# Transposing normalised tiles by DMA instead of by the tensor array: layernorm, dilated attention and a gated feed-forward on one core

## Chip, cores, metric

One NeuronCore of a Trainium2 chip. The metric is the device time of one execution in microseconds (us); medians over several executions are quoted, with lowest and highest; these take in the runs classed as slow (one of the run with the array kept busy, two of the run with the early load alone), the ratios do not. "Before" and "after" are the kernel without and with the change.

## The reference

```python
S, D, H, F = 2048, 448, 16, 1792                  # bfloat16
xn = layernorm(x)                                 # (S, D)
q, k, v = split(xn @ wqkv)                        # 16 heads of 28
# each position attends to 8 positions: itself and 2, 4 .. 14 before it
s = softmax(q . k * 28**-0.5, masked) @ v @ wo
g = silu(gelu(xn @ w1 + b1) @ w2 + b2)
return x + s * g
```

The rows are held as even positions and then odd ones, so that the dilated window becomes a plain one. They are worked in four chunks of 512 (four tiles of 128 rows each).

## The kernel before

All matmuls that read `xn` take it from a buffer with features on the partitions. So every normalised tile (`xnb`, 128 rows by 512 columns, four buffers used in turn) is transposed by the array (TensorE, PE in profiles) into a PSUM buffer (`pT`) and copied into one feature-major buffer `xnT`.

```python
LEAD = 8                                          # columns of zeros ahead of xnT
...                                               # loads, all issued from the SP queue
nc.sync.dma_start(b1t[:], B_b1.rearrange("(m f) -> f m", f=P))
for c0, c1 in ((0, F // 2), (F // 2, F)):
    ...                                           # half of w1
    if c0 == 0:
        nc.sync.dma_start(x_sb[1][:, :, :], dram_rows(x_par, 4, 4))
...                                               # w2, b2, x_sb[2], x_sb[3]
for g in range(4):
    for h in range(4):                            # sixteen small pieces of wo
        r = (4 * g + h) * DH
        nc.sync.dma_start(wo[32 * h + 1:32 * h + 1 + DH, g, :], A_wo[r:r + DH, :])

def ln_tr(t):                                     # four array transposes of one tile
    pT = psB.tile([P, KT, P], BF16, name="pT", tag="B")
    for kt in range(KT):
        nc.tensor.transpose(pT[:, kt, :], xnb[t % 4][:, kt * P:(kt + 1) * P], ident[:])
    return pT

def ln_put(t, pT, copy):
    copy(xnT[:, :, LEAD + t * P:LEAD + (t + 1) * P], pT[:, :, :])

def feed_forward_1(c, ps, wos):                   # chunk c; seven pairs of blocks, k = 0 .. 6
    ...
    for k in range(0, MT // 2, 2):
        ...                                       # matmuls and gelu of pairs k and k + 1
        if k in (2, 4):
            if c + 1 < NC:                        # transposes of the NEXT chunk
                for j in (k - 2, k - 1):
                    ln_put(nx + j, ln_tr(nx + j), nc.vector.tensor_copy)
            ...
        for _ in range(2):                        # output projections of finished tiles
            if k >= (2 if c == 3 else 4) and wos:
                wo_job(wos.pop(0))
```

The order of the array, VectorE, ScalarE and GpSimd is fixed by hand to the order of the program. The queue on the sync engine (SP), which issues nearly all DMAs, is left to the scheduler.

The softmax here doesn't subtract the row's maximum and nothing guards it: scores larger than these inputs give would overflow.

Of the kernel before, what the change touches and what calls it, by code (L numbers as in the profile page):

```python
# [15 lines left out]
S, D, H, DH, F = 2048, 448, 16, 28, 1792  # L16
P = 128
NT = S // P
NC = 4
# [3 lines left out]
QB = 121  # L23
QW = 122
NB = 17
LEAD = 8
LQ = LEAD + S + 24
SCALE = 1.0 / math.sqrt(DH)
EPS = 1e-5
NG = 12  # L30
# [3 lines left out]
def kernel(  # L34
# [14 lines left out]
    nc = tc.nc  # L49
    assert tuple(A_x.shape) == (1, S, D)  # L50
    x_par = A_x.rearrange("b (s two) d -> two (b s) d", two=2)
    out_par = out.rearrange("b (s two) d -> two (b s) d", two=2)

    def dram_rows(par, t0, n):
        cls, r = divmod(t0 * P, S // 2)
        return par[cls, r:r + n * P, :].rearrange("(t p) d -> p t d", p=P)
# [7 lines left out]
    x_sb = [big.tile([P, 4, D], BF16, name=f"x_{c}") for c in range(NC)]  # L64
# [36 lines left out]
    for dst, c0, c1 in ((wv, 2 * D, 3 * D), (wraw, 0, 2 * D)):  # L101
        nc.sync.dma_start(dst[:, 0:3, 0:c1 - c0], A_wqkv[0:384, c0:c1].rearrange("(k p) f -> p k f", p=P))
        nc.sync.dma_start(dst[:64, 3, 0:c1 - c0], A_wqkv[384:448, c0:c1])
    nc.sync.dma_start(b1t[:], B_b1.rearrange("(m f) -> f m", f=P))
    for c0, c1 in ((0, F // 2), (F // 2, F)):
        nc.sync.dma_start(w1[:, 0:3, c0:c1], B_w1[0:384, c0:c1].rearrange("(k p) f -> p k f", p=P))  # L106
        for r in (0, 64):
            nc.sync.dma_start(w1[r:r + 64, 3, c0:c1], B_w1[384:448, c0:c1])
        if c0 == 0:
            nc.sync.dma_start(x_sb[1][:, :, :], dram_rows(x_par, 4, 4))  # L110
    nc.sync.dma_start(w2[:, :, :], B_w2.rearrange("(m p) c -> p m c", p=P))
    nc.sync.dma_start(b2bc[:], B_b2.rearrange("(o d) -> o d", o=1).to_broadcast((P, D)))
    nc.sync.dma_start(x_sb[2][:, :, :], dram_rows(x_par, 8, 4))
# [49 lines left out]
    def ln_apply(t):  # L163
        nc.vector.tensor_scalar(xnb[t % 4][:, 0:D], xt(t), mv[:, t, 0:1], rstd[:, t:t + 1],
                                op0=ALU.subtract, op1=ALU.mult)

        nc.vector.tensor_copy(xnb[t % 4][:, D:512], xnb[t % 4][:, D - 64:D])

    def ln_tr(t):
        pT = psB.tile([P, KT, P], BF16, name="pT", tag="B")  # L170
        for kt in range(KT):
            nc.tensor.transpose(pT[:, kt, :], xnb[t % 4][:, kt * P:(kt + 1) * P], ident[:])
        return pT

    def ln_put(t, pT, copy):
        copy(xnT[:, :, LEAD + t * P:LEAD + (t + 1) * P], pT[:, :, :])


    def qk_weights(which, kt):
# [124 lines left out]
    def qk_unit(b, between=lambda: None):  # L304
# [10 lines left out]
        for p2 in range(2):  # L315
# [4 lines left out]
            if p2 == 0:  # L320
                between()
        return E

    def av_unit(b, E):
        psO = psB.tile([P, 4, P], F32, name="psO", tag="B")
        for g in range(4):
            for h in range(4):
                nc.tensor.matmul(psO[32 * h:32 * h + 32, g, 0:QW], vw[:, b, 4 * g + h, :],  # L328
                                 E[:, h, g, 0:QW], start=True, stop=True)
        n = min(QB, S - QB * b)  # L330
        den = work.tile([P, 4, QB], F32, name="den", tag="den", bufs=2)
        nc.vector.stream_shuffle(den[:, :, 0:n], psO[:, :, 0:n], [0] * 32)  # L332

        def norm():
            nc.scalar.activation(den[:, :, 0:n], den[:, :, 0:n], ACT.Ln)  # L335
            nc.scalar.activation(den[:, :, 0:n], den[:, :, 0:n], ACT.Exp, scale=-1.0)  # L336
            nc.vector.tensor_tensor(out=oT[:, :, QB * b:QB * b + n], in0=psO[:, :, 0:n],  # L337
                                    in1=den[:, :, 0:n], op=ALU.mult)
        return norm
# [3 lines left out]
    def busy(n):  # L343

        ps = psB.tile([P, CH], F32, name="ps_w", tag="B")
        for _ in range(n):
            nc.tensor.matmul(ps[:, :], wz[:, 0:P], wz[:, :], start=True, stop=True)

    def feed_forward_1(c, ps, wos):

        nc.scalar.preload_act_table_set(SET_GELU)
        nx = 4 * (c + 1)
        gelu(0, ps)
        for k in range(0, MT // 2, 2):
            if k:
                ps = ffn1_even(c, k)
                gelu(k, ps)
            if k + 1 < MT // 2:
                ps = ffn1_odd(c, k + 1)
                gelu(k + 1, ps)  # L360
            if c + 2 < NC and k < 4:
                ln_stats(nx + 4 + k)
                ln_stats(nx + 5 + k)
            if k in (2, 4):
                if c + 1 < NC:
                    for j in (k - 2, k - 1):
                        ln_put(nx + j, ln_tr(nx + j), nc.vector.tensor_copy)
                if c:
                    silu_job(4 * (c - 1) + k - 2)
                    silu_job(4 * (c - 1) + k - 1)  # L370
            for _ in range(2):
                if k >= (2 if c == 3 else 4) and wos:
                    wo_job(wos.pop(0))
        nc.scalar.preload_act_table_set(SET_EXP)
        if c + 2 < NC:
            ln_rstd(nx + 4, 4)


    with tc.manual_schedule(engines={ENG.PE, ENG.Activation, ENG.DVE, ENG.Pool}):
        nc.scalar.preload_act_table_set(SET_EXP)  # L380
        busy(8)
        ln_stats(0)
        ln_rstd(0, 1)
        ln_stats(1)
        ln_rstd(1, 1)
        ln_apply(0)
        pT = [ln_tr(0)]
        ln_put(0, pT[0], nc.scalar.copy)
        ln_stats(2)
        ln_rstd(2, 1)  # L390
        ln_apply(1)
        pT.append(ln_tr(1))
        v0 = v_mm(0)
        ln_put(1, pT[1], nc.scalar.copy)
        ln_stats(3)
        ln_rstd(3, 1)
        v_put(0, v0)
        ln_apply(2)
        pT.append(ln_tr(2))
        v1 = v_mm(1)  # L400
        ln_put(2, pT[2], nc.scalar.copy)
        v_put(1, v1)
        ln_apply(3)
        pT.append(ln_tr(3))
        v2 = v_mm(2)
        ln_put(3, pT[3], nc.scalar.copy)
        v_put(2, v2)
        v_job(3)
        for which in range(2):
            for kt in range(KT):  # L410
                qk_weights(which, kt)
        y_sb = work.tile([P, 4, D + 4], F32, name="y", tag="stage", bufs=1)
        late_constants()
        for g in range(4):
            q_job(0, g)
            if g == 3:
                ln_stats(7)
                ln_rstd(4, 4)
            else:
                ln_stats(4 + g)  # L420
            k_job(0, g)
        ps = ffn1_even(0, 0)
        for t in range(4, 8):
            ln_apply(t)

        units = iter(range(NB))
        for c in range(3):
            feed_forward_1(c, ps, [[], [0, 1], [2, 3, 4, 5]][c])
            n = c + 1
            beside = [lambda: q_job(n, 3), lambda: k_job(n, 3), lambda: v_job(4 * n), lambda: v_job(4 * n + 1)]  # L430
            if c == 2:
                beside[1] = lambda: (k_job(3, 3), v_job(12))
                beside[2] = lambda: v_job(13)
                beside[3] = lambda: v_job(14)
            for g in range(3):
                q_job(n, g)
                k_job(n, g, nc.vector.tensor_copy)
            norm = lambda: None
            for i in range(4):
                b = next(units)  # L440
                E = qk_unit(b)
                norm()
                ffn2_job(4 * c + i)
                beside[i]()
                if n + 1 < NC:
                    ln_apply(4 * n + 4 + i)
                norm = av_unit(b, E)
            b = next(units)
            va, vb = 4 * n + 2 + (c == 2), 4 * n + 3 + (c == 2)
            E = qk_unit(b, lambda: v_job(va))  # L450
            v_job(vb)
            norm()
            ps = ffn1_even(n, 0)
            norm = av_unit(b, E)
            norm()
        feed_forward_1(3, ps, [6, 7, 8, 9, 10])
        ffn2_job(12)
        E = qk_unit(15)
        g12 = silu_exp_job(12)
        ffn2_job(13)  # L460
        g12()
        s11 = wo_mm(11)
        norm = av_unit(15, E)
        wo_put(11, s11)
        E = qk_unit(16)
        g13 = silu_exp_job(13)
        norm()
        y14 = ffn2_job(14, False)
        s12 = wo_mm(12)
        norm = av_unit(16, E)  # L470
        g13()
        ffn2_put(14, y14)
        wo_put(12, s12)
        s13 = wo_mm(13)
        norm()
        nc.scalar.preload_act_table_set(SET_GELU)
        wo_put(13, s13)
        silu_job(14)
        y15 = ffn2_job(15, False)
        s14 = wo_mm(14)  # L480
        s15 = wo_mm(15)
        ffn2_put(15, y15)
        wo_put(14, s14)
        silu_job(15)
        wo_put(15, s15)
# [29 lines left out]
```

## Time and profile before

| | before |
|---|---|
| time, median of the first 3 runs | 177.59 us |
| span of the profiled run | 176.4 us |
| array (PE) busy | 163.9 us, 93% |
| VectorE (DVE) / ScalarE (ACT) busy | 120.0 / 124.7 us |
| mean granted array clock | 0.997 |

Read it together with the chain that ended last, which the prediction shows: on average the array has little slack, and where it has some, a ScalarE chain sets the pace. The time is 1 to 2 us more than the span (178.06 against 176.4 in the profiled run). The kernel before also has late runs, at about 180 us with a clock of 0.988; some were classed as slow and are left out of the ratios. The two in the first round of experiments (wo behind, half of wo, array kept busy, chunk 1 by the array) were classed as fast and stay in, which makes those four ratios up to 0.3% too low.

### The profile page before, as it was taken

How to read it: one execution, taken by the hardware profiler on the slowest of the kernel's cores; microseconds unless marked ns; L12 is line 12 of the kernel's file. 1: busy time of each engine (PE TensorE's matmuls, PEld its weight loads, DVE VectorE, ACT ScalarE, POOL GpSimd, SP SyncE). 2: the span in 40 equal slices, each digit the busy share in tenths (PEclk: the TensorE clock that was granted, in tenths of full speed). 3: DMA queues.
4: the chain of work that ended last, by engine and by line, in shares of the span. 5: the costliest groups of instructions: out<-in, count | busy, mean ns of one | idle time of the engine just before them, and what ended most of it. 6: DMA issues, size and time to landing. Idle time of an engine off the chain costs nothing.

```text
span 176.4 us, 3278 instructions
## 1 busy us (share of the span) xinstructions
PE 163.9 (93%) x1324; PEld 75.6 (43%) x1324; DVE 120.0 (68%) x269; ACT 124.7 (71%) x196; POOL 4.5 (3%) x16
## 2 busy tenths in 40 slices
PE   7698999999999989999999989999999999999480
PEld 2343344444454334445454335444555434445140
DVE  6854846667886655977886415987677413978693
ACT  3853397646889699646879699534788699978650
POOL 6030000000000000000000000000000000000000
PEclk9999999999999999999999999999999999999998
DMA  5999972000000000100000000210000000120011
GB/s 145 232 239 320 362 245 50 3 0 4 0 4 0 0 0 4 52 0 4 0 0 6 0 0 0 73 34 0 4 0 0 4 2 0 52 78 30 0 52 52
DMA packets 10991, 9.03 MB, mean 51 GB/s; under 512 B 2593, under 2 KB 10977, under 8 KB 10977
## 3 DMA queue, kind: packets, MB, share of 16 engines
q1 hardware_dynamic: 10688, 8.61, 16.6%
q10 hardware_dynamic: 288, 0.23, 0.4%
q8 instruction: 10, 0.16, 0.4%
q14 instruction: 5, 0.03, 0.1%
HBM read 7.00 MB, written 1.84 MB: 50 GB/s over the span
## 4 chain that ended last, share of the span: by engine, by line
PE 68%; ACT 15%; DVE 7%; SPq 4%; DMA 3%; issue 2%; DVEq 0%
PE ps_y L257 23%; PE ps_h L224 13%; PE ps_qk L188 13%; PE ps_s L288 6%; ACT E L317 4%; PE S L312 3%; PE ps_v L203 3%; DMA x<-in_A_x_dram 3%; PE ps_h L233 3%; ACT hT L239 3%; ACT den L336 2%; PE psO L328 2%; SPq L106 2%; ACT den L335 2%; DVE den L332 2%
## 5 line engine op out<-in xcount | busy, mean ns | idle before, releaser
L317 ACT ACTIVATE E<-S 128x976 bf16<-128x976 f32 x34 | 32.0, 985 | 19.6 <-PE S L312 18.7
L257 PE MATMUL ps_y<-w,hT 128*128 128x448 bf16 x224 | 45.1, 353 | 0.7 <-DVE y L264 0.7
L224 PE MATMUL ps_h<-xnT,w 128*128 128x512 bf16 x168 | 40.3, 380 | 1.5 <-ACT hT L239 1.5
L239 ACT ACTIVATE hT<-ps_h,b1f 128x512 bf16<-128x512 f32 x56 | 33.9, 708 | 2.6 <-PE ps_h L233 2.2
L188 PE MATMUL ps_qk<-xnT,wqk 128*128 128x512 bf16 x128 | 29.4, 379 | 0.6 <-DVE qT L191 0.6
L257 PEld LDWEIGHTS <-hT 128*128 128x128 bf16 x224 | 20.8, 98 | 20.2 <-issue 0.9
L319 DVE TENSOR_TENSOR E<-E,mk_gen 128x976 bf16<-128x976 bf16 x30 | 19.9, 666 | 7.6 <-ACT E L317 7.6
L224 PEld LDWEIGHTS <-w 128*128 128x128 bf16 x168 | 15.4, 98 | 21.4 <-issue 5.7
L337 DVE TENSOR_TENSOR oT<-psO,den 128x484 bf16<-128x484 f32 (+1 forms) x17 | 11.2, 661 | 12.7 <-ACT den L336 12.7
L188 PEld LDWEIGHTS <-wqk 128*128 128x128 bf16 x128 | 12.4, 98 | 15.5 <-issue 1.4
L269 DVE SCALAR_TENSOR_TENSOR g<-th,y 128x448 bf16<-128x448 bf16 x14 | 8.2, 621 | 14.1 <-ACT th L268 14.1
L203 PE MATMUL ps_v<-wv,xnT 128*128 128x448 bf16 x68 | 15.2, 353 | 0.1
L288 PE MATMUL ps_s<-wo,oT 128*128 128x448 bf16 x64 | 13.8, 353 | 1.6 <-DVE oT L337 1.6
L335 ACT ACTIVATE den<-den 128x484 f32<-128x484 f32 (+1 forms) x17 | 10.4, 610 | 5.4 <-DVE den L332 5.4
L191 DVE CAST qT<-ps_qk 128x512 bf16<-128x512 f32 x16 | 10.9, 682 | 3.5 <-PE ps_qk L188 3.5
L156 DVE BATCH_NORM_STATS2 st<-x 128x6 f32<-128x448 bf16 x16 | 9.8, 610 | 5.0 <-DMA x<-in_A_x_dram 5.0
L208 ACT CAST vw<-ps_v 128x448 bf16<-128x448 f32 x17 | 9.1, 536 | 3.9 <-PE ps_v L203 3.8
L332 DVE STREAM_SHUFFLE den<-psO 128x484 f32<-128x484 f32 (+1 forms) x17 | 11.8, 696 | 0.0
L233 PE MATMUL ps_h<-xnT,w 64*128 64x512 bf16 x56 | 10.5, 384 | 0.4
L336 ACT ACTIVATE den<-den 128x484 f32<-128x484 f32 (+1 forms) x17 | 10.3, 605 | 0.5
L264 DVE TENSOR_TENSOR y<-ps_y,b2bc 128x448 f32<-128x448 f32 x16 | 9.9, 618 | 0.9 <-PE ps_y L257 0.8
L294 DVE SCALAR_TENSOR_TENSOR sg<-ps_s,g 128x448 bf16<-128x448 f32 x16 | 9.9, 618 | 0.2
(60 smaller groups left out, 126.5 us busy)
## 6 DMA issues: line engine op xcount, KB each, us to landing
out_dram<-o_t SPq DMA_DIRECT2D x16, 112.0 KB
w<-in_B_w_dram SPq DMA_DIRECT2D x1, 1568.0 KB
w<-in_B_w_dram SPq DMA_DIRECT2D x2, 672.0 KB
x<-in_A_x_dram SPq DMA_DIRECT2D x3, 448.0 KB
wraw<-in_A_wqkv_dram SPq DMA_DIRECT2D x1, 672.0 KB
w<-in_B_w_dram SPq DMA_DIRECT2D x4, 112.0 KB
wo<-in_A_wo_dram SPq DMA_DIRECT2D x16, 24.5 KB
wv<-in_A_wqkv_dram SPq DMA_DIRECT2D x1, 336.0 KB
```

Of the source, the lines that this page charges most:

```text
L188: nc.tensor.matmul(ps[:, :], wqk[:, kt, 16 * which + 4 * g:16 * which + 4 * g + 4, :], xnT[:, kt, LEAD + c * CH:LEAD + (c + 1) * CH], star ...
L203: nc.tensor.matmul(ps[:, :], xnT[:, kt, o:o + P], wv[:, kt, :], start=(kt == 0), stop=(kt == KT - 1))
L224: nc.tensor.matmul(ps[i][:, :], w1[:, kt, m * P:(m + 1) * P], xnT[:, kt, LEAD + c * CH:LEAD + (c + 1) * CH], start=(first and kt == 0), st ...
L233: nc.tensor.matmul(ps[i][:, :], w1[r, 3, m * P:(m + 1) * P], xnT[r, 3, LEAD + c * CH:LEAD + (c + 1) * CH], start=first, stop=not first)
L239: nc.scalar.activation(hT[:, m, :], ps[i][:, :], ACT.Gelu_apprx_tanh, bias=b1f[:, m:m + 1])
L257: nc.tensor.matmul(ps[:, :], hT[:, m, tt * P:(tt + 1) * P], w2[:, m, :], start=(m == 0), stop=(m == MT - 1))
L288: nc.tensor.matmul(ps[:, :], oT[:, g, t * P:(t + 1) * P], wo[:, g, :], start=(g == 0), stop=(g == 3))
L317: nc.scalar.activation(ev, Sp[p2][:, :, :, 0:QW], ACT.Exp, scale=SCALE)
L319: nc.vector.tensor_tensor(out=ev, in0=ev, in1=mkb, op=ALU.mult)
L332: nc.vector.stream_shuffle(den[:, :, 0:n], psO[:, :, 0:n], [0] * 32)
L335: nc.scalar.activation(den[:, :, 0:n], den[:, :, 0:n], ACT.Ln)
L336: nc.scalar.activation(den[:, :, 0:n], den[:, :, 0:n], ACT.Exp, scale=-1.0)
```

## The change

Intent: take the 48 transposes of chunks 1 to 3 off the array and the 12 copies off VectorE, and let idle DMA engines do both (in the page of before, under 0.3 busy in every slice from 31 us on). Tiles of chunk 0 stay as they were. Three smaller edits go with it: the load of x tiles 4 to 7 comes earlier, three warm-up matmuls are added, and one normalisation in the tail is moved ahead of a sigmoid.

```diff
-LEAD = 8
-LQ = LEAD + S + 24
+LEAD = 16
+LQ = LEAD + S + 16
...
+    nc.sync.dma_start(x_sb[1][:, :, :], dram_rows(x_par, 4, 4))
     nc.sync.dma_start(b1t[:], B_b1.rearrange("(m f) -> f m", f=P))
...
-        if c0 == 0:
-            nc.sync.dma_start(x_sb[1][:, :, :], dram_rows(x_par, 4, 4))
...
+    def ln_dma(t):
+        nc.sync.dma_start_transpose(xnT[:, :, LEAD + t * P:LEAD + (t + 1) * P], xnb[t % 4][:, :])
...
             if k in (2, 4):
-                if c + 1 < NC:
-                    for j in (k - 2, k - 1):
-                        ln_put(nx + j, ln_tr(nx + j), nc.vector.tensor_copy)
...
-        busy(8)
+        busy(9)
...
         pT = [ln_tr(0)]
+        busy(2)
...
         for t in range(4, 8):
             ln_apply(t)
+            ln_dma(t)
...
                 if n + 1 < NC:
                     ln_apply(4 * n + 4 + i)
+                    ln_dma(4 * n + 4 + i)
...
         E = qk_unit(16)
+        norm()
         g13 = silu_exp_job(13)
-        norm()
```

(The other lines of the diff only drop an argument of `ln_put`. What the wider LEAD is for, no run here shows.)

More of the change, by code (lines that the diff above doesn't have):

```diff
@@ L173, in ln_tr, with ln_put @@
         return pT
-    def ln_put(t, pT, copy):
-        copy(xnT[:, :, LEAD + t * P:LEAD + (t + 1) * P], pT[:, :, :])
+    def ln_put(t, pT):
+        nc.scalar.copy(xnT[:, :, LEAD + t * P:LEAD + (t + 1) * P], pT[:, :, :])
+    def ln_dma(t):
+        nc.sync.dma_start_transpose(xnT[:, :, LEAD + t * P:LEAD + (t + 1) * P], xnb[t % 4][:, :])
     def qk_weights(which, kt):
@@ L387 @@
         pT = [ln_tr(0)]
-        ln_put(0, pT[0], nc.scalar.copy)
+        busy(2)
+        ln_put(0, pT[0])
         ln_stats(2)
@@ L393 @@
         v0 = v_mm(0)
-        ln_put(1, pT[1], nc.scalar.copy)
+        ln_put(1, pT[1])
         ln_stats(3)
@@ L400 @@
         v1 = v_mm(1)
-        ln_put(2, pT[2], nc.scalar.copy)
+        ln_put(2, pT[2])
         v_put(1, v1)
@@ L405 @@
         v2 = v_mm(2)
-        ln_put(3, pT[3], nc.scalar.copy)
+        ln_put(3, pT[3])
         v_put(2, v2)
```

## The prediction

> **What bounds the kernel now.** I read the page first: the engine shares and the 40 slices. They say that the array is busy everywhere, at a granted clock of full speed.
>
> ```profile
> PE 163.9 (93%) x1324; PEld 75.6 (43%) x1324; DVE 120.0 (68%) x269; ACT 124.7 (71%) x196; POOL 4.5 (3%) x16
> PEclk9999999999999999999999999999999999999998
> DMA  5999972000000000100000000210000000120011
> ```
>
> The reader is to see two things. TensorE (PE) has almost no slack on average, and the DMA engines are saturated for the first 25 us or so and nearly idle after that. So work taken off the array should count, and transfers added late are cheap in bandwidth. Next, the chain that ended last, in order of time. Where it names a transpose (pT), that transpose is on the path; where the transpose is missing, something else set the pace. These pieces (start, us, what) are from feed-forward stages 0 and 1:
>
> ```profile
> 25.25 0.45 PE pT L172 x8
> 28.93 0.45 PE pT L172 x8
> 31.00 5.29 PE ps_qk L188 x24
> ...
> 61.28 2.43 ACT hT L239 x4
> 63.71 0.04 issue
> 63.75 1.46 PE ps_h L224 x6
> 65.21 0.54 PE ps_h L233 x4
> 65.75 1.40 PE ps_h L224 x6
> 67.15 0.45 PE pT L172 x8
> ```
>
> There are six groups of eight transposes (12 tiles by four). Each takes 0.45 us. Four are in the chain: 25.25, 28.93, 67.15 and 106.88. The first group of stage 1 ran at 62.35, while the array had to wait until 63.75 for a gelu on ScalarE anyway; the first group of stage 2 is missing from the chain for the same reason. The query-key projections of chunk 1, the first readers of the transposed tiles 4 to 7, start at 31.00.
>
> Last, the timeline of the DMA-issuing queue (SP), because the new transposes are issued from it, and the chain around the first wait for input:
>
> ```profile
> 17.41 0.57 SPq L113 DMA_DIRECT2D x<-in_A_x_dram  x1
> 18.03 1.77 SPq L114 DMA_DIRECT2D x<-in_A_x_dram  x1
> 19.92 10.17 SPq L134 DMA_DIRECT2D wo<-in_A_wo_dram  x16
> ```
>
> ```profile
> 10.22 5.18 DMA x<-in_A_x_dram
> ...
> 16.90 1.89 PE ps_qk L188 x8
> ```
>
> SP issues strictly in the program's order (inputs, weights, then sixteen small pieces of wo), and it is not free until 19.92 + 10.17 = 30.09 us. This row decides my prediction. The last two lines show the second block of x being waited for: the array stood 0.57 us before 16.90.
>
> [...] This trace has a median of 383 ns for issuing a wo piece[...]; no row here shows a transpose. [...] This trace has a median of 219 ns for one on the array, and 56 ns each in a row of eight. [...] the warm-up matmuls of 512 columns follow each other every 0.43 us; later ones need 1.40 / 6 = 0.23.
>
> **The change, part by part.**
>
> Removed: 48 array transposes, 6 groups x 0.45 = 2.7 us of PE. Two groups lie in waits for gelu, so 4 x 0.45 = 1.8 us are on the path. Also removed: 12 VectorE copies of 415 ns (5 us of DVE work, in no piece of the chain, with VectorE 68% busy), which I count as zero, and six PSUM turns, also zero, since the chain names no wait for them.
>
> Moved: the load of x tiles 4 to 7 now goes ahead of b1 and the first half of w1. It should land well before its statistics are due, so the 0.57 us hole before 16.90 goes. The first half of w1 then lands about when x did, 15.4 us, and is needed at about 18.0: no new wait. The total of bytes ahead of wo is the same and the engines are saturated, so SP still comes free at about 30.1.
>
> Moved in the tail: the normalisation of unit 15 goes ahead of the three ScalarE steps of the sigmoid of tile 13. In the chain these are 162.02 to 163.70, after them den 163.70 to 164.84, and only then the product that frees a PSUM buffer. After the swap the product comes at about 163.2 instead of 164.86, den of unit 16 is shuffled while the sigmoid runs, and the sum y of tile 14, which starts the last ffn2 at 167.21, comes after sigmoid (164.9) plus g 0.62 and y 0.62, at about 166.1. Gain 1.1 us.
>
> Added: a ninth warm-up matmul and two more behind the first transpose. They fill array idle time (0.58 us before 5.35, 0.80 us before 6.59): within 0.1 us, zero.
>
> Added: 12 DMA transposes of 128x512. For chunks 2 and 3 they are issued one per attention unit, some 4 us apart, at 37 to 53 and 77 to 93 us, with SP idle (its next business is at 71.90), and are read from about 70 and 112 us: hidden, unless one takes over 10 us.
>
> For chunk 1 they are not hidden. The normalised tiles are ready at about 20 to 22 us, but SP is busy with wo to 30.1 us, and program order puts the transposes behind that. I take 1.0 us to issue each[...] and 2.0 us from issue to landing (estimate from the first x tiles, issued at 0.81 and used at 3.44). Then the last lands at 30.1 + 4 x 1.0 + 2.0 = 36.1. The projections of chunk 1 need all four, since one matmul reads 512 columns. Without the hole and the two groups, the array would be ready at 31.0 - 0.57 - 0.9 = 29.5, so it stands for about 6.6 us. Against before, the start of the projections goes from 31.0 to 36.1: +5.1. This swallows the 0.57 and the first two groups. The array falls to half speed in that gap; the eight warm-up matmuls took 3.4 us at half speed, so some 1.7 us are lost.
>
> Sum: +5.1 + 1.7 - 0.9 (the groups of 67.15 and 106.88) - 1.1 (tail) = +4.8, or 182.4 us.
>
> **The rivals.**
>
> A. Blocked queue, as above: 182.4. For it: the strict order of SP's timeline, even behind stalled issues, and that the diff leaves wo in its place. Within it, 0.6 us an issue and 1.5 to landing would give 34.0 and about 180.3; 2 us an issue would give 40 and about 186[...].
>
> B. Transposes of chunk 1 issued in time: if the scheduler lets them slip in front of wo (at 20 to 22 us), everything is hidden and the gains add up: 0.57 + 1.8 + 1.1 = 3.5, or 174.1 us. For it: the load of x was brought forward, which makes sense only if somebody gains from early tiles. Against it: nothing in the trace has ever left program order on SP. I give it one in five.
>
> C. The gain is hidden: ScalarE paces the feed-forward stages (gelu with tanh of the previous chunk), so the array waits where it transposed. The chain supports this for two groups of six; if for all, B shrinks to 175.9 and A grows by 0.9.
>
> **Range and chances.** With A at about four in five, centred on 182.4 with a tail both ways, and B near 174 to 176, I say 181.5 us, with 174.0 to 188.0. Slower by over 2% is above 181.1: about two thirds of A, 0.54. Faster by over 2% is below 174.0: half of B and little else, 0.12. Within 2%: 0.34.
>
> **What would show it.** Right: a DMA transpose on SP after the last wo piece, at about 30 us; a wait of several us of the projections (the weight load or the matmul of L188's counterpart) for the DMA of xnT; slow matmuls just behind it; two pT groups gone from the later chain; a last ffn2 starting sooner after its predecessor. Wrong: transposes standing ahead of wo on SP, or an SP free well before 30 us; no wait of the array between 28 and 36; landing times under 1 us. The most probable way to be wrong is the order on SP, then the duration of one transpose.

## The result, and the profile after

After: 184.25 us (183.68 to 185.66, 4 runs) against 177.93 us for the kernel before in the same rounds. The ratio is 1.038, 95% interval 1.030 to 1.046: slower. A ratio here is the mean of one kernel's fast runs over the mean of the other's of the same rounds, so not quite the ratio of the medians quoted.

The page of the kernel after, its engine shares and its row of granted clock:

```profile
PE 164.3 (90%) x1279; PEld 73.6 (40%) x1279; DVE 116.1 (64%) x257; ACT 124.6 (68%) x196; POOL 4.5 (2%) x16
PEclk9999999559999999999999999999999999999999
```

The array runs 45 instructions fewer (48 transposes out, three warm-ups in) and yet is busy longer, with two slices of the span at half clock. Those slices are about 32 to 41 us. The SP queue just ahead of them (start, us, queue, line, what was issued):

```profile
19.10 10.40 SPq L133 DMA_DIRECT2D wo<-in_A_wo_dram  x16
29.61 5.22 SPq L178 DMA_TRANSPOSE xnT<-xnb  x4
```

The transposes of chunk 1 stand behind all sixteen pieces of wo, although their tiles were ready by 21.4 us in this trace. The chain that ended last, in this stretch:

```profile
29.61 1.30 SPq L178
...
31.02 1.20 SPq L178
...
32.31 1.22 SPq L178
...
33.62 2.48 DMA xnT<-xnb
36.09 0.14 issue
36.23 7.98 PE ps_qk L190 x24
44.21 0.33 PE S L314 x16
```

SP and then the DMA have taken the place of the array in the chain. The projections of chunk 1 start at 36.23 instead of 31.00, after a wait that the list of waits puts at 6.9 us, and the same 24 matmuls take 7.98 us instead of 5.29. Why, the array's weight loads of this stretch show (start, us, engine, line):

```profile
36.61 0.15 PEld L190 LDWEIGHTS <-wqk 128*128 128x128 bf16 x1 [0.28 <-issue]
37.03 0.15 PEld L190 LDWEIGHTS <-wqk 128*128 128x128 bf16 x1 [0.28 <-issue]
...
41.30 0.15 PEld L190 LDWEIGHTS <-wqk 128*128 128x128 bf16 x1 [0.28 <-issue]
41.67 2.04 PEld L190 LDWEIGHTS <-wqk 128*128 128x128 bf16 x10 [0.22 <-issue]
```

They follow each other every 0.43 us until 41.3, and after that ten take 2.04 us: half speed for some 5.4 us, then full speed. Later, in feed-forward stage 1, the transposes are gone from the chain as intended (before, 0.45 us of pT stood between the last two of these pieces):

```profile
71.68 1.46 PE ps_h L226 x6
...
73.68 1.40 PE ps_h L226 x6
75.08 1.51 PE ps_s L290 x8
```

And the tail. First before, then after, from the chains: ScalarE's sigmoid (se), its logarithm and exponential of the softmax sums (den), VectorE's product with them (oT) and its sum y, and the last product with w2, called ffn2 (ps_y).

```profile
162.02 0.47 ACT se L275
...
163.70 0.51 ACT den L335
...
164.86 0.04 DVE oT L337
...
166.62 0.54 DVE y L264
...
167.21 2.81 PE ps_y L257 x14
```

```profile
169.27 0.50 ACT den L337
...
170.40 0.47 ACT se L277
...
172.66 0.63 DVE y L266
173.33 2.81 PE ps_y L259 x14
```

The scores of unit 16, the last unit of attention, start at 159.80 before and 167.05 after. From there to the last ffn2 it was 7.41 us and is 6.28.

### The profile page after: what moved, and what is told of

Same layout as the page of the kernel before. It is cut to its first block, busy times and chain, and to the rows that moved or that the text cites. A ratio compares the mean times of both kernels' runs of the same rounds, so it can differ in the third digit from the quotient of the medians.

```text
span 182.2 us, 3201 instructions
## 1 busy us (share of the span) xinstructions
PE 164.3 (90%) x1279; PEld 73.6 (40%) x1279; DVE 116.1 (64%) x257; ACT 124.6 (68%) x196; POOL 4.5 (2%) x16
## 4 chain that ended last, share of the span: by engine, by line
PE 59%; ACT 15%; SPq 11%; DMA 6%; DVE 5%; issue 2%; DVEq 0%
PE ps_y L259 23%; PE ps_qk L190 13%; PE ps_h L226 8%; PE ps_s L290 6%; DMA x<-in_A_x_dram 5%; ACT E L319 4%; PE S L314 3%; PE ps_v L205 3%; ACT hT L241 3%; SPq L107 2%; ACT den L338 2%; PE psO L330 2%; ACT den L337 2%; SPq L178 2%; SPq L133 2%
## 5 line engine op out<-in xcount | busy, mean ns | idle before, releaser
L259 PE MATMUL ps_y<-w,hT 128*128 128x448 bf16 x224 | 45.1, 353 | 1.2 <-DVE y L266 1.2
L190 PE MATMUL ps_qk<-xnT,wqk 128*128 128x512 bf16 x128 | 32.1, 404 | 6.9 <-DMA xnT<-xnb 6.9
L190 PEld LDWEIGHTS <-wqk 128*128 128x128 bf16 x128 | 13.0, 103 | 23.8 <-issue 11.4
```

The source lines that it names most:

```text
L190: nc.tensor.matmul(ps[:, :], wqk[:, kt, 16 * which + 4 * g:16 * which + 4 * g + 4, :], xnT[:, kt, LEAD + c * CH:LEAD + (c + 1) * CH], star ...
L259: nc.tensor.matmul(ps[:, :], hT[:, m, tt * P:(tt + 1) * P], w2[:, m, :], start=(m == 0), stop=(m == MT - 1))
```

## The experiments

Theory Q: the whole loss is SP's order, with wo ahead of the transposes of chunk 1; everything else in the change gains or is neutral. Rival T: a DMA transpose is slow or disturbing in itself. All kernels gave correct results, and all but one profile (said below) are of fast runs. The runs are told in the order of the argument. "Faster" here means an interval clear of 1; the verdict on record, which asks for 2%, is faster only for the runs with the hole filled, and unclear or same for the others.

### wo behind the transposes

```diff
-    for g in range(4):
-        for h in range(4):
-            ...  nc.sync.dma_start(wo[...], A_wo[...])
+    def wo_load(g0, g1): ...                      # the same loop
...
-    with tc.manual_schedule(engines={ENG.PE, ENG.Activation, ENG.DVE, ENG.Pool}):
+    with tc.manual_schedule(engines={ENG.PE, ENG.Activation, ENG.DVE, ENG.Pool, ENG.SP}):
...
         for t in range(4, 8):
             ln_apply(t)
             ln_dma(t)
+        wo_load(0, 4)
```

> The changed kernel with one thing moved: the sixteen pieces of wo are issued behind the four transposes of chunk 1 (SP order fixed to the program's). Theory Q (the loss is SP's order alone): the transposes are issued from about 20 us, land before the array asks at 29.3, no wait, no cold array; the gains of 0.57 + 1.8 + 1.1 us appear and the time is about 174 (ratio to before 0.98). Rival T (a transpose is slow in itself, or waits in the DMA engines behind the inputs, which land until about 26 us): the last one lands at 31 or later, the array waits 2 us or more and the time is 176 or more.

Measured: 174.34 us (174.21 to 174.50, 4 runs), ratio 0.977, interval 0.971 to 0.982: faster than before. The SP queue, then the array, in this run:

```profile
20.07 6.54 SPq L179 DMA_TRANSPOSE xnT<-xnb  x4
26.66 6.97 SPq L134 DMA_DIRECT2D wo<-in_A_wo_dram  x16
```

```profile
29.09 0.39 PE L236 MATMUL ps_h<-xnT,w 64*128 64x512 bf16 x2
29.41 5.35 PE L191 MATMUL ps_qk<-xnT,wqk 128*128 128x512 bf16 x24
```

The projections follow the feed-forward without a gap, and at full speed. One move in the order of issue turns a loss of 3.8% into a gain of 2.3%, with every transpose still in place. The edit also fixes the order on SP by hand; in the two traces the order is otherwise the same, and the run with wo on GpSimd below, which does not fix it, gains too. That is theory Q, and within 0.3 us of what rival B of the prediction made of the time.

### Half of wo behind

```diff
+    wo_load(0, 2)                                 # where wo was
...
             ln_dma(t)
+        wo_load(2, 4)
```

> Only the last eight pieces of wo are issued behind the transposes of chunk 1. Theory Q: eight issues of 0.42 us come out of the way, so the last transpose lands 3.4 us earlier, at about 32.7, and the wait of the array shrinks from 6.9 to about 3.5 us; the time falls by 3.4 to about 180.9 if the array still goes cold, by up to 6.1 to 178.2 if so short a wait leaves it warm. Rival T: landing hardly moves, time near 184.

Measured: 181.14 us (179.93 to 182.12), ratio 1.014. The direction holds, but the transposes land at 34.45, not 32.7: SP came free at 27.29 instead of 26.1, because its eighth piece of wo waits for a block of x that lands only at 26.91 here, and the last transpose took 3.09 us from issue to landing. So the first pieces of wo are held by the inputs (the first eight took 6.88 us to issue), and only the last ones cost 0.43 us each (in the kernel after, from 26.1 us on). The array waited 5.3 us and still went cold, but for 3.0 us only: the projections took 6.84 us.

### The array kept busy in its wait

```diff
+            if c == 0:
+                busy(28)
             for g in range(3):
                 q_job(n, g)
```

> The changed kernel with 28 matmuls of zeros (6 us at full speed) put in front of the projections of chunk 1, so that the array is busy during its wait. If the slow matmuls behind the wait come from the idleness: the wait for the transposes is as before, the 24 projections take 5.3 instead of 8.0 us, and the time is 2.7 us less, about 181.6. Rival (the transposes or their traffic slow the array): the projections stay at 8.0 us and the time at 184.

Measured: 182.87 us (181.64 to 184.59, the last a slow run), ratio 1.022. The array in the profiled run:

```profile
29.23 6.22 PE L349 MATMUL ps_w<-wz 128*128 128x512 bf16 x28
37.57 5.34 PE L190 MATMUL ps_qk<-xnT,wqk 128*128 128x512 bf16 x24 [2.12 <-DMA xnT<-xnb]
```

The projections are back at 5.34 us, with the same transposes and the same wait for them. So the slow matmuls come from the idleness, not from the transposes. The time fell by less than 2.7 us since in this run the transposes landed 1.3 us later (SP began them at 31.00 instead of 29.61).

### Chunk 1 by the array, chunks 2 and 3 by DMA

```diff
         for t in range(4, 8):
             ln_apply(t)
-            ln_dma(t)
...
+                if c == 0:
+                    for j in (k - 2, k - 1):
+                        nc.vector.tensor_copy(xnT[..., tile 4 + j], ln_tr(4 + j)[:, :, :])
```

> The changed kernel with chunk 1 transposed by the array and copied by VectorE as in the kernel before; chunks 2 and 3 by DMA. Theory Q (all the loss is in chunk 1, chunks 2 and 3 are hidden): no wait, before less 0.57 (x early), 0.9 (two groups of chunks 2 and 3 that were on the path) and 1.1 (tail) = about 175.3, ratio 0.986. Rival T (DMA transposes cost something wherever they are): 177 or more.

Measured: 175.42 us (175.35 to 175.45), ratio 0.983, interval 0.977 to 0.988. The loss is in chunk 1 alone.

### Transposes of chunks 2 and 3 doubled

```diff
     def ln_dma(t):
+        if t >= 8:
+            nc.sync.dma_start_transpose(scr[t % 4][:, :, :], xnb[t % 4][:, :])
         nc.sync.dma_start_transpose(xnT[...], xnb[t % 4][:, :])
```

(on top of the kernel with wo behind)

> The run with wo behind, plus a second transpose of every tile of chunks 2 and 3 into a scratch tile, issued ahead of the real one. Theory Q (in chunks 2 and 3 a transpose costs nothing, they are hidden by 10 us or more): same time, 174.3. Rival (each costs the array or VectorE something, by SBUF traffic or late buffers): eight more would show as 0.5 us or more.

Measured: 174.41 us (174.06 to 174.46) against 174.34. Eight more transposes cost nothing measurable there: the longest waits of the array are the same in both profiles (2.5, 1.3 and 1.2 us). The two runs are of different chips, and their ratios to before are 0.980 and 0.977 with intervals that overlap, so a few tenths of a us would not show. Rival T in any larger size is out for chunks 2 and 3.

### wo issued from GpSimd

```diff
-    ... nc.sync.dma_start(wo[...], A_wo[...])     # in the loads
...
         late_constants()
+        wo_load(0, 4)                             # nc.gpsimd.dma_start
```

> The changed kernel with wo issued from GpSimd's queue, behind its mask constants (from about 13 us), and so out of SP's order, while its data still go through the same DMA engines early. Theory Q (what costs is the place in SP's order, not wo's data): the transposes are issued from 20 us and time and wait are as in the run with wo behind, about 174.3. Rival (the wo transfers in the DMA engines delay the transposes' data): the array waits and the time is over 176.

Measured: 175.66 us (175.02 to 176.49), ratio 0.988: between the two. SP starts the transposes at 20.34, but needs 8.15 us for the four, and the chain shows:

```profile
27.28 3.94 DMA xnT<-xnb
31.22 0.14 issue
31.35 5.34 PE ps_qk L191 x24
```

So the order on SP is by far the larger part (175.66 against 184.25), and there is a second, smaller limit: transfers that are under way. With wo's data moving early on another queue, the block of x for chunk 2 landed at 27.1 instead of 24.6 us in the kernel after, the transposes came later, and the array waited 1.8 us. That wo's data are the reason is argued, not shown: the profile is of the slowest of the four runs, and with wo behind the same block landed as late as 26.7 us (in the profile of the next section). My expectation put this down as an either-or; it is both.

### The hole where transposes lay hidden

In stages 1 and 2 the array waits for a gelu just where a group of transposes was. Two output projections fit there:

```diff
-                if k >= (2 if c == 3 else 4) and wos:
+                if k >= 2 and wos:
```

(on top of the kernel with wo behind)

> The run with wo behind, with the first two output projections of stages 1 and 2 put in front of the feed-forward block that waits for a gelu, where the two hidden groups of transposes had stood (the array waits 2.5 us there in both stages together). If that hole is real slack that the change emptied but could not use: 2.4 us less, about 172. If the projections are then late themselves (VectorE's gate or PSUM buffers), same time, 174.3.

Measured: 172.31 us (172.22 to 173.10), ratio 0.970. The array in stage 1, first with wo behind only, then with the hole filled:

```profile
59.53 1.47 PE L227 MATMUL ps_h<-xnT,w 128*128 128x512 bf16 x6
62.24 1.46 PE L227 MATMUL ps_h<-xnT,w 128*128 128x512 bf16 x6 [1.24 <-ACT hT L242]
```

```profile
60.14 1.47 PE L227 MATMUL ps_h<-xnT,w 128*128 128x512 bf16 x6
61.45 1.68 PE L291 MATMUL ps_s<-wo,oT 128*128 128x448 bf16 x8
62.96 1.46 PE L227 MATMUL ps_h<-xnT,w 128*128 128x512 bf16 x6
```

The wait is gone there, and of the 2.5 us of such waits 0.9 us are left further on. So two groups of transposes out of six had been free, as the prediction's third rival said of them; removing those gained nothing until other work moved in.

### Is the landing of chunk 1 still tight?

The profile of that run, the slowest of its four (173.10 us), showed 0.9 us of waiting for the transposes of chunk 1. I ran the kernel again, and with one load more moved behind them:

```diff
-    nc.sync.dma_start(x_sb[3][:, :, :], dram_rows(x_par, 12, 4))   # in the loads
...
             ln_dma(t)
+        nc.sync.dma_start(x_sb[3][:, :, :], dram_rows(x_par, 12, 4))
         wo_load(0, 4)
```

> The kernel of the hole-filling run once more, for a comparison on the same chip: about 172.3, with a wait for the transposes of chunk 1 of 0 to 1 us, as its profile showed.

> The same with the load of x tiles 12 to 15 (448 KB, needed only at about 60 us) issued behind the transposes of chunk 1 too. If what now times their landing is the backlog of inputs in the DMA engines ahead of them: 448 KB at the 350 GB/s of this stretch is 1.3 us, the transposes land so much earlier, no wait is left, and the time is the same or up to 0.9 us less. If their landing is set by their own issue and transfer: no change in landing, the wait stays.

Measured on the same chip: 172.35 us (172.27 to 172.71, 6 runs) and 172.29 us (172.12 to 172.43, 5 runs), ratios 0.969 and 0.968. In these two profiles neither array waits for xnT in a way that the list of waits names. So the times do not settle whether the backlog sets the landing. The SP queue tells more: the four issues took 5.89 us with the load of x moved and 7.14 us without, and ended at 25.8 instead of 27.9. Of these 2.1 us, 0.9 come from an earlier start and 1.25 from shorter issues, close to the 1.3 expected from the backlog; that is one profile of each. There was no wait left to gain from, and the version is as good with or without this edit.

### Parts of the change alone, on the kernel before

Only the swap in the tail:

```diff
         E = qk_unit(16)
+        norm()
         g13 = silu_exp_job(13)
-        norm()
```

> The kernel before with nothing but the swap in the tail. Working of the prediction: 1.1 us less than before, ratio 0.994. Rival: the tail is bound by the last vector operations, ratio 1.000.

Measured: 176.81 us (176.15 to 177.35, 6 runs) against 177.89, ratio 0.994, interval 0.991 to 0.998. As expected.

Only the early load of x:

```diff
+    nc.sync.dma_start(x_sb[1][:, :, :], dram_rows(x_par, 4, 4))
     nc.sync.dma_start(b1t[:], ...)
...
-        if c0 == 0:
-            nc.sync.dma_start(x_sb[1][:, :, :], dram_rows(x_par, 4, 4))
```

> The kernel before with nothing but the load of x tiles 4 to 7 brought forward. Working of the prediction: the 0.57 us hole of the array before 16.90 goes and nothing else waits, 0.6 us less, ratio 0.997. Rival: the first half of w1 then comes late and the hole moves behind the projections, ratio 1.000 or more.

Measured: 178.03 us (177.16 to 180.40, 6 runs) against 178.29, ratio 0.998, interval 0.993 to 1.002. The size fits, but it is not clear of zero. Its profile fell on a late run (180.40 us, state slow), so nothing is read from it but how such a run starts:

```profile
7.01 1.70 PE L202 MATMUL ps_v<-wv,xnT 128*128 128x448 bf16 x4
```

Four matmuls that take 0.92 us in the fast profile of before take 1.70 here, and again at 8.94. This array was still at about half speed at 7 to 9 us, though the granted clock is given as 1.00 from 4 to 12 us.

Only the three added warm-up matmuls:

```diff
-        busy(8)
+        busy(9)
...
         pT = [ln_tr(0)]
+        busy(2)
```

> The kernel before with nothing but the three added warm-up matmuls. The prediction counted them as zero. But the kernel before has shown about one run in four at 180.0 to 180.4 instead of 177.3 to 178.9, the profile that fell on such a run has its array at half speed until about 11 us, and none of 27 runs of the kernels with wo or chunk 1 put right, which have the added matmuls, was so late. If the matmuls are why: no run at 180, fast runs as before (178 or up to 0.3 less), ratio of fast runs near 1.000. If not: one or two of the five or six runs at 180 again.

Measured: 178.10 us (177.20 to 179.70, 6 runs) against 178.66, ratio 0.997, interval 0.991 to 1.003. Two of the six runs, 179.15 and 179.70, had a clock of 0.989. So these matmuls alone do not keep the late runs away, and my reading of why the good kernels had none falls. The record points to the tail. In the late profile of the run with the early load, the page has the granted clock at 0.7 and 0.8 in the two slices from 165.4 to 174.3 us, and all matmuls with w2 (ps_y) together at 46.7 us instead of 45.1; that is 1.6 us, where its span exceeds that of before by 2.4 us. And a clock of 0.988 or 0.989 fell on 22 of 64 runs of kernels with the old tail, but on none of 37 with the swap in the tail, alone or with wo or chunk 1 put right (lowest 0.992). Only six of the 37 have the swap alone, so this is likely, not shown.

## Why the prediction was right

Rival A, which carried four fifths of the weight, is what happened. Its terms, against the two profiled runs:

| step | predicted | measured |
|---|---|---|
| SP free for the transposes | 30.1 us | 29.61 |
| four issues | 4 x 1.0 us | 5.22 us, so 1.31 each |
| end of the last issue to landing | 2.0 us | 36.09 - (29.61 + 5.22) = 1.26 |
| projections of chunk 1 start | 36.1 (+5.1) | 36.23 (+5.23) |
| the array's wait | 6.6 us | 6.89 |
| lost at half speed | 1.7 us | 7.98 - 5.29 = 2.69 |
| two later groups of transposes | -0.9 | stage 1: 6.97 to 6.53; stage 2: 8.60 to 8.14: -0.90 |
| tail | -1.1 | 7.41 to 6.28: -1.13 |

The stages in the seventh row are taken from the feed-forward block that waits for gelu to the projections of the next chunk. Two terms that I had not seen: the projections of chunk 3 took 5.40 instead of 5.18 us (+0.22), and the span ended 0.3 us sooner after the last vector operation. The sum is 5.23 + 2.69 - 0.90 + 0.22 - 1.13 - 0.3 = +5.8, which is 182.2 less 176.4.

**The queue.** The order on SP, read off one row of the timeline of the kernel before, was the step on which all else hung. The runs with wo behind, with half of it behind, and with wo on another queue show that it is the cause: 174.34, 181.14 and 175.66 us.

**What was mis-sized.** The cost of half speed: 2.69 us instead of 1.7. I took the 3.4 us of the eight warm-up matmuls for the length of a warm-up; here half speed lasted 5.4 us after the wait. The term differs by run (1.5 us in the run with half of wo behind), and keeping the array busy removes it. The granted clock was at half from 31.4 to 41.6 us in the kernel after: 10.2 us, beginning 2.0 us after the last matmul. With half of wo behind, the weight loads followed each other every 0.43 us only until 37.5, some 3.0 us after the wait of 5.3. That the array would fall to half speed in its wait was my estimate; the trace of before could not show it, as its longest wait of the array is 1.6 us. What fixes when the clock falls and when it returns was not tested.

Issue and landing were each off, by +0.31 us four times and by -0.74 us, and SP was free 0.5 us sooner; these errors cancelled, which is luck. The 1.0 us for an issue was my estimate, with no DMA transpose in the trace of before to take it from. In the kernel after one held SP for 1.20 us (median of 12; 1.19 to 1.76; a piece of wo 0.38), and the last of chunk 1 landed 2.48 us after its issue began, with the engines' mean busy share at 0.57. Issued at 20 to 21 us instead, while inputs were still landing, four took 5.89 to 8.15 us instead of 5.22 (the runs with wo behind or on GpSimd).

**The headline.** 181.5 us lies below the 182.4 of rival A because a fifth of the weight lay on B. The measured 184.25 is 1.9 us above rival A: 1.0 is the difference of the two sums, nearly all of it the half speed; 0.5 is that the profiled run of before took 178.06 us, while the prediction starts from the median, 177.59; and 0.3 is that the median after lies above the profiled 183.91.

**Rival B** was wrong as a forecast of this kernel, and right about what the change is worth without the queue: 174.1 predicted, 174.34 measured once wo was moved. **Rival C** held for the two groups it was seen in, and no more.

**The copies off VectorE** and the warm-ups were counted as zero. No run contradicts that: the terms above add up without them, and the warm-ups alone gave no clear change.

## What to carry to other kernels

Before moving work from a compute engine to a DMA, read the issuing queue's timeline at the moment when the work would be issued. SP issued in order in these traces, and the transposes paid for the sixteen pieces of wo ahead of them (10.40 us), though those were needed later; moving them behind was worth 9.9 us (184.25 to 174.34). Loads that are needed late belong behind those needed early, also where the DMA engines have bandwidth to spare (here 56 to 67 GB/s just ahead of the transposes, from 28 to 29.6 us, against 370 in the busiest slice). And a wait of several us can cost the array more than its length: after 6.9 and 5.3 us (kernel after, half of wo behind) it came out at half speed and lost 2.7 and 1.5 us more, after 2.1 and 1.8 us (array kept busy, wo on GpSimd) it did not. Removing the transposes that already lay in a wait gained nothing until output projections were put there (174.34 to 172.31 us).
